# Retention of two sequences side by side in a fused retention and feed-forward kernel

## Chip, cores, metric

One NeuronCore of a Trainium2 chip. The metric is the device time of one execution in microseconds (us). An interval is a 95% interval of the ratio of two kernels.

## The reference

Eight sequences of 576 tokens, 8 heads of 64, go through retention; the result, 4608 tokens of 512 numbers, goes through a feed-forward layer with a squared ReLU.

```python
scores = q @ k.T / sqrt(64)              # per sequence and head
ret    = scores * gamma ** (i - j)       # for i >= j, else 0
x      = ret @ v                         # heads side by side: (4608, 512)
h      = maximum(x @ w_in, 0)            # (4608, 2048)
out    = (h * h) @ w_out                 # (4608, 512)
```

## The kernel before

A chunk is 128 tokens of one sequence (the fifth is 64). TensorE transposes k and q (`turn`), multiplies them (`scores`), and adds up the result from within the chunk and from a running state (`retain_a`, `retain_b`, `retain_c`). All of this runs in 64*64 or 64*128 tiles of TensorE. The results fill blocks of 512 tokens, and each block after the first goes through the first feed-forward product in 28 steps (`ffn_in`: four times seven block products, whose sums VectorE forms). A step is four matmul calls, which the profile shows as 8 records of 128x256: each call leaves two records. The steps of older blocks stand between the parts of retention:

```python
# main loop, from the sixth chunk on
retain_a(i - 1)
turn(i)              # k and q of chunk i
ffn(i - 1, 0)        # some 3 or 4 feed-forward steps
retain_b(i - 1)
scores(i)
retain_c(i - 1)
ffn(i - 1, 1)        # some 3 or 4 more
load(i + 3)
```

In `turn`, ScalarE copies kT out of PSUM, and VectorE takes out qT and multiplies it by the decay in the same instruction:

```python
nc.vector.tensor_tensor(to, p[:, :n_h, j, :, :], dq[...], op=ALU.mult)
```

The second product (`o_a`, `o_b`, `o_c`) follows when all retention is done.

## Time and profile before

| | before |
|---|---|
| time, median | 995.3 us |
| span of the profiled run | 991.7 us |
| TensorE busy / idle | 973.5 / 18.2 us |
| first block's products end | 104.3 us |
| second product starts at about | 560 us |
| time at half TensorE clock | 3.9 us |

The prediction shows the page, the stretches and a timeline. The view of TensorE's waits adds the following (what waited, for what: us in total, times, the longest). A wait for "issue" is one that no semaphore explains.

```profile
PE x_ps L436 <- ACT u_sb L474: 3.4, 4, 1.8
...
PE x_ps L471 <- issue: 1.3, 1, 1.3
...
PE t_ps L387 <- DVE q_ld L377: 0.6, 1, 0.6
```

### The profile page before, as it was taken

The numbers are of one execution on the slowest core, as the hardware profiler recorded it, in microseconds if no ns is written. First come the engines' busy times: TensorE is split into PE (matmuls) and PEld (weight loads), VectorE is DVE, ScalarE is ACT, GpSimd is POOL, SyncE is SP. The second block draws the span as 40 slices with busy tenths as digits, with TensorE's granted clock in tenths as the row PEclk, the third lists the DMA queues.
The fourth block names the chain that finished last, engine by engine and source line by source line (L and its number), as shares of the span: only waits on it lengthen the run. The fifth ranks groups of instructions, "written<-read, shape, count | busy, mean of one in ns | idle before, by whom it ended". The sixth has DMA issues, their size and how long they took to land.

```text
span 991.7 us, 24441 instructions
## 1 busy us (share of the span) xinstructions
PE 973.5 (98%) x10532; PEld 869.5 (88%) x10532; DVE 748.6 (75%) x1427; ACT 190.4 (19%) x462; POOL 81.6 (8%) x85
## 2 busy tenths in 40 slices
PE   7899999999999999999999999999999999999998
PEld 7655688888888888888888889999999999999998
DVE  4688696567878888897886777777777777777765
ACT  3444222222222222223221010000000000000000
POOL 3100011111111111111111000000000000000000
PEclk9999999999999999999999999999999999999999
DMA  9984657665696878769458999675673757556351
GB/s 205 250 239 143 174 172 208 162 175 176 187 311 199 223 234 260 224 209 283 142 212 297 404 389 348 235 283 163 230 268 148 265 197 270 192 213 216 126 212 44
DMA packets 187676, 220.40 MB, mean 222 GB/s; under 512 B 119216, under 2 KB 137648, under 8 KB 178608
## 3 DMA queue, kind: packets, MB, share of 16 engines
q1 hardware_dynamic: 185456, 218.31, 67.8%
q8 instruction: 83, 1.36, 0.6%
q10 hardware_dynamic: 2112, 0.52, 0.2%
q14 instruction: 25, 0.20, 0.1%
HBM read 129.41 MB, written 89.39 MB: 221 GB/s over the span
## 4 chain that ended last, share of the span: by engine, by line
PE 91%; DVE 5%; DMA 1%; SPq 1%; issue 1%; ACT 1%; DVEq 0%; ACTq 0%
PE o_b L866 17%; PE h_b L595 16%; PE o_c L866 11%; PE o_a L866 11%; PE h_a L595 10%; PE h_c L595 10%; PE h_ps L559 5%; PE x_ps L436 3%; PE t_ps L387 2%; PE sc_ps L415 2%; PE x_ps L471 2%; DVE room L602 1%; PE u_ps L439 1%; DMA w<-in_moe_w_in_dram 1%; DMA w<-in_moe_w_out_dram 0%
## 5 line engine op out<-in xcount | busy, mean ns | idle before, releaser
L595 PE MATMUL h_b<-room,w 128*128 128x256 f32 x736 | 177.2, 383 | 1.2 <-DVE room L520 0.9
L595 PEld LDWEIGHTS h_b<-room,w 128*128 128x128 f32 x736 | 137.2, 190 | 21.4 <-PE t_ps L387 1.1
L866 PE MATMUL o_b<-w,room 128*128 128x128 f32 x1168 | 144.5, 275 | 0.2 <-DVE room L817 0.2
L866 PEld LDWEIGHTS o_b<-w,room 128*128 128x128 f32 x1168 | 137.2, 192 | 0.5 <-DVE room L817 0.4
L866 PE MATMUL o_c<-w,room 128*128 128x128 f32 x1008 | 123.0, 275 | 0.0
L866 PEld LDWEIGHTS o_c<-w,room 128*128 128x128 f32 x1008 | 117.7, 192 | 0.0
L595 PE MATMUL h_c<-room,w 128*128 128x256 f32 x480 | 114.4, 381 | 0.0
L595 PE MATMUL h_a<-room,w 128*128 128x256 f32 x448 | 107.6, 383 | 0.0
L595 PEld LDWEIGHTS h_c<-room,w 128*128 128x128 f32 x480 | 90.4, 190 | 12.6
L595 PEld LDWEIGHTS h_a<-room,w 128*128 128x128 f32 x448 | 83.7, 190 | 11.8
L866 PE MATMUL o_a<-w,a 128*128 128x128 f32 x688 | 85.6, 275 | 0.0
L866 PEld LDWEIGHTS o_a<-w,a 128*128 128x128 f32 x688 | 81.2, 192 | 0.1
L612 POOL TENSOR_TENSOR room<-room 128x512 f32<-128x512 f32 x32 | 35.2, 1100 | 438.2 <-ACT room L611 370.6
L602 DVE SCALAR_TENSOR_TENSOR room<-room 128x512 f32<-128x512 f32 x96 | 68.1, 710 | 3.3
L880 ACT COPY r<-o_a 128x128 f32<-128x128 f32 x53 | 14.1, 266 | 271.7 <-PE o_a L866 241.2
L559 PE MATMUL h_ps<-room,w 128*128 128x512 f32 (+1 forms) x160 | 60.1, 526 | 2.5 <-DVE w L228 1.7
L614 DVE TENSOR_TENSOR room<-h_b,room 128x512 f32<-128x512 f32 x32 | 22.1, 690 | 46.9 <-PE h_b L595 46.9
L436 PEld LDWEIGHTS x_ps<-ret,v_ld 64*64 64x64 f32 x1152 | 40.4, 136 | 15.9 <-issue 11.7
L436 PE MATMUL x_ps<-ret,v_ld 64*64 64x64 f32 x1152 | 50.0, 226 | 3.5 <-ACT u_sb L474 3.4
L559 PEld LDWEIGHTS h_ps<-room,w 128*128 128x128 f32 x160 | 30.3, 196 | 24.6 <-issue 19.1
L424 POOL TENSOR_TENSOR v_ld<-v_ld,dv 128x512 f32<-128x512 f32 (+1 forms) x40 | 42.8, 1075 | 63.5 <-DMA v_ld<-in_v_dram 58.6
L876 DVE TENSOR_TENSOR small<-o_b,small 128x128 f32<-128x128 f32 x62 | 18.1, 292 | 38.4 <-PE o_b L866 38.4
(109 smaller groups left out, 1377.4 us busy)
## 6 DMA issues: line engine op xcount, KB each, us to landing
g_dram<-room SPq DMA_DIRECT2D x32, 1792.0 KB, 7.7
a<-g_dram SPq DMA_DIRECT2D x43, 1024.0 KB, 7.1
room<-g_dram SPq DMA_DIRECT2D x20, 1024.0 KB, 6.4
w<-w_dram SPq DMA_DIRECT2D x7, 1792.0 KB, 13.0
out_dram<-room SPq DMA_DIRECT2D x17, 512.0 KB, 3.4
w<-in_moe_w_in_dram SPq DMA_DIRECT2D x16, 512.0 KB, 6.1
w<-in_moe_w_out_dram SPq DMA_DIRECT2D x16, 512.0 KB, 4.1
v_ld<-in_v_dram SPq DMA_DIRECT2D x31, 256.0 KB, 4.4
```

The lines of the kernel that those rows point to most:

```text
L387: nc.tensor.transpose(p[:, h, j, hp, :], loaded[i][j][rows(h), 2 * hp:2 * hp + 2, :], ident[rows(h), rows(h)])
L415: nc.tensor.matmul(sc[e][rows(h), hp, :], lhsT=kT[rows(e), hp, t], rhs=qT[rows(e), hp, t], start=True, stop=True, skip_group_check=True)
L424: nc.gpsimd.tensor_tensor(vs[:cs], vs[:cs], dv[:cs, :, ci:ci + 1].to_broadcast([cs, H, D]), op=ALU.mult)
L436: own.append(lambda hp=hp, e=e, b=b: nc.tensor.matmul(x_at(hp, b, h), lhsT=s["vs"][rows(h), 2 * hp + b, :], rhs=s["ret"][rows(h), e, hp, : ...
L471: nc.tensor.matmul(x_at(hp, b, h), lhsT=u[rows(e), hp, :], rhs=s["qT"][rows(e), hp, CH * h:CH * h + CH], start=clears(b, hp // 2), stop=Fa ...
L559: nc.tensor.matmul(p.rearrange("p h t -> p (h t)"), lhsT=w[:, c, :], rhs=xT[0][:, c, lo * HT:hi * HT], start=(c == 0), stop=(c == N_DM - 1))
L595: nc.tensor.matmul(p[:, mm, :], lhsT=w[:, c, :], rhs=xs[n][right][:, c, :], start=(j in OPENS and mm == 0 and c == 0), stop=(j in CLOSES a ...
L602: nc.vector.scalar_tensor_tensor(t, t, 0.0, t, op0=ALU.max, op1=ALU.mult)
L612: nc.gpsimd.tensor_tensor(g["A11"], g["A11"], g["A11"], op=ALU.mult)
L614: nc.vector.tensor_tensor(g["A22"], p, p15, op=ALU.add)
L866: nc.tensor.matmul(p, lhsT=s["lefts"][left][:, m, :], rhs=w_out[j][:, m, WO_SLOT[right], :], start=(i in OPENS and m == 0), stop=(i in CLO ...
L876: nc.vector.tensor_tensor(s["u2"], p, s["p1"], op=ALU.add)
```

## The change

The intent is to switch between retention and feed-forward half as often. A "visit" is the same chunk of two sequences; their results share PSUM banks, so evictions are half as many and twice as wide. q is multiplied by its decay per token before the transposes, so that no table of decays by column is needed and qT is a plain copy. The order of the tokens in a block changes, so the output is stored in pieces of 128 or 64 rows. The core of the diff:

```diff
-    chunks = [(b, ci, ci * C, min(C, S - ci * C)) for b in range(B) for ci in range(NCH)]
+    visits = [(b, ci, ci * C, min(C, S - ci * C)) for b in range(0, B, 2) for ci in range(NCH)]
...
-                nc.vector.tensor_tensor(to, p[:, :n_h, j, :, :], dq[...], op=ALU.mult)
+            (nc.vector.tensor_copy if j == 0 and i < N_EARLY else nc.scalar.copy)(to, p[:, :n_h, j, :, :])
...
+    for i in range(N_EARLY, N_V + 1):
+        if i > N_EARLY:
+            if i < N_V:
+                turn(i, 0)               # first sequence of visit i
+            retain_a(i - 1)              # both sequences
+            if i < N_V:
+                turn(i, 1)               # second sequence
+            ffn(i - 1, 0)
+        if i + 1 < N_V:
+            load(i + 1, "q")
+        if i > N_EARLY:
+            retain_b(i - 1)              # both
+        if i < N_V:
+            scores(i)                    # both
+        if i > N_EARLY:
+            retain_c(i - 1)              # both
+        if i + 1 < N_V:
+            load(i + 1, "k")
+            load(i + 1, "v")
+        ffn(i - 1, 1)
+        if i + 1 < N_V:
+            scale_q(i + 1, nc.vector)
```

Cut: the early visits, which get the same order by hand; first-block products at half width, which go; and the stores.

## The prediction

> **What bounds the kernel now.** I read the page's sums and slices first, then the chain that ended last, then the stretches, the waits of TensorE, and last a timeline of one round of the middle part.
>
> ```profile
> span 991.7 us, 24441 instructions
> PE 973.5 (98%) x10532; PEld 869.5 (88%) x10532; DVE 748.6 (75%) x1427; ACT 190.4 (19%) x462; POOL 81.6 (8%) x85
> PE 91%; DVE 5%; DMA 1%; SPq 1%; issue 1%; ACT 1%; DVEq 0%; ACTq 0%
> ```
>
> TensorE is busy for 98% of the span and carries 91% of the chain that ended last. It waits for almost nothing; the table of stretches (us, TensorE busy) says where the 18 us of idle time lie:
>
> ```profile
> 0.00:46.00 46.00, 35.98 (x739) 30.86 (x740) 23.28 (x44) 18.09 (x38) 12.14 (x20) 0.96 0.91 219
> 104.00:537.00 433.00, 428.86 (x5369) 364.22 (x5368) 344.67 (x572) 106.88 (x235) 60.91 (x57) 1.00 0.70 212
> 560.00:992.00 432.00, 428.00 (x3684) 423.55 (x3683) 315.83 (x704) 36.23 (x130) 3.12 (x3) 1.00 0.63 228
> ```
>
> 10 us are in the start. The middle, where retention of later chunks is woven into the first feed-forward products, idles 4 us of 433; VectorE (third figure) is at 80% there. From 560 us on only the second product runs, which the change leaves alone but for its stores. So nothing can be won by removing waits; only TensorE's own work, or its order, can move the time. Here is one round of the middle (start us, us, engine, line):
>
> ```profile
> 305.16 0.23 PE L436 MATMUL x_ps<-ret,v_ld 64*64 64x64 f32 x2
> 305.17 0.23 PE L439 MATMUL u_ps<-v_ld,k_ld 64*64 64x64 f32 x2
> 305.32 1.99 PE L595 MATMUL h_b<-room,w 128*128 128x256 f32 x8
> 307.16 1.89 PE L595 MATMUL h_c<-room,w 128*128 128x256 f32 x8
> 308.88 1.89 PE L595 MATMUL h_b<-room,w 128*128 128x256 f32 x8
> 310.70 0.27 PE L436 MATMUL x_ps<-ret,v_ld 64*64 64x64 f32 x2
> ...
> 311.33 0.46 PE L387 MATMUL t_ps<-ident,k_ld 64*128 64x64 f32 x4
> 311.62 0.41 PE L387 MATMUL t_ps<-ident,q_ld 64*128 64x64 f32 x4
> 311.97 1.99 PE L595 MATMUL h_a<-room,w 128*128 128x256 f32 x8
> ```
>
> The reader is to see two things. A feed-forward group between its like takes 1.72 us start to start (307.16 to 308.88), but 1.84 just after retention and 1.82 just before it. And the transposes of q start 0.29 us after those of k, waiting for nobody: they read q as it was loaded. Now VectorE over the same moment; the three feed-forward groups ended at about 310.77:
>
> ```profile
> 307.36 0.69 DVE L614 TENSOR_TENSOR room<-h_b,room 128x512 f32<-128x512 f32 x1 [1.71 <-PE h_b L595]
> 308.08 0.69 DVE L602 SCALAR_TENSOR_TENSOR room<-room 128x512 f32<-128x512 f32 x1
> 308.69 0.42 DVE L214 TENSOR_SCALAR w<-w 128x512 uint32<-128x512 uint32 x1
> ...
> 311.02 0.68 DVE L621 TENSOR_TENSOR room<-h_b,room 128x512 f32<-128x512 f32 x1
> 311.74 0.69 DVE L602 SCALAR_TENSOR_TENSOR room<-room 128x512 f32<-128x512 f32 x1
> 312.35 0.68 DVE L533 TENSOR_TENSOR room<-room 128x512 f32<-128x512 f32 x1
> 312.95 0.68 DVE L225 TENSOR_TENSOR w<-w,w 128x512 f32<-128x512 f32 x1
> 313.55 0.42 DVE L397 TENSOR_TENSOR qT<-t_ps,dq 128x256 f32<-128x256 f32 x1
> ```
>
> VectorE is never the bound, but it runs **behind** TensorE: it finishes the work of the last group 2.9 us after that group ended, and only then gets to q (L397). Nobody minds today, because L397 comes after the transposes and its result is wanted only after the next 3 or 4 groups.
>
> [...] retention runs in 64*64 and 64*128 tiles, the feed-forward in 128*128, and each border costs about 0.1 us on either side. [...] The trace has one such wait already, at the very start (0.6 us, transposes for the scaling of q at L377). [...] the copy of kT at 26.11 us starts when the transposes of q end, 0.3 us after those of k.
>
> **The change part by part.** (1) **Fewer borders.** Before, 35 chunks after the early ones have two calls of feed-forward steps each: 70 rounds of "out of 128*128 and back". After, 18 visits (2 to 19) have two each, 36 at most. 34 rounds go. One round costs 0.10 (group before) + 0.12 (group after) + about 0.09 (the last retention matmul starts 0.15 us before the feed-forward, where its cadence is 0.06) + 0.04 (the first pair) = 0.35 us. Gain: 34 x 0.35 = **12 us**. The switch between transposes and 64*64 products is as frequent as before per sequence pair (turn, retain, turn), so it gives nothing.
>
> (2) **Same TensorE work.** The count of transposes, scores, products and state updates per token is unchanged, and TensorE is the bound: 0 us.
>
> (3) **Half as many, twice as wide evictions.** ScalarE and VectorE save fixed costs (a 128x256 copy takes 375 ns, a 128x512 one 585), but ScalarE is busy 19% and VectorE isn't the bound: 0 us. ScalarE takes over the eviction of qT, 585 ns each.
>
> (4) **q scaled by tokens, on VectorE, ahead of the transposes.** This is the part that I weigh most. The multiply by decay moves from behind the transposes (L397, 686 ns) to in front of them (a 128x512 TENSOR_TENSOR out of SBUF, about 690 ns as L377 at the start took 0.69), and it is issued after the last step of the second feed-forward call, just ahead of the next visit's transposes. Over 30 turns between 110 and 520 us I took the moment when VectorE was done with everything ahead of L397, from the end of the last feed-forward group: 0.1 to 4.7 us, median 2.4. By the order of the changed code I worked out on which product each second call ends: mostly on the fifth of seven (7 of 17), where VectorE is least behind: an addition, a square and one piece of the conversion of w_out, as at 307.36, done at 309.1, which is 1.8 us after the group's end at 307.3. Scaling then ends at 1.8 + 0.65 = 2.4 to 2.5; the transposes of q could have begun at 0.3. Stall: 2.1 to 2.2 us. For the other ten, 2.4 + 0.65 - 0.3, about 2.8 us. Mean 2.5 us x 17 visits (3 to 19) = **43 us**, all on TensorE's path[...].
>
> (5) **One buffer for q, two for k and v.** k of the next visit but one can load only when the current visit's last state update is done, six transfers in a row of 0.6 to 1.3 us issue each, 4.8 us median to landing. The first half lands about 7 us later; a half of 7 steps gives 12 us, but the halves beside the 64-token visits have 3 or 4 steps, 5 to 7 us. Estimate: 3 visits x 1.5 us more = 4 us, on top of (4).
>
> (6) **One transpose buffer, used twice a visit.** The second half's transposes wait for two ScalarE copies of the first half, 1.25 us; the products between take 2 x 0.63 us. About even: estimate 0.1 us x 17 = 2 us.
>
> (7) **Start.** x of the first block is ready at about 41 us now; I estimate 34 after, from the chain transposes, evictions, scores, mask of four sequence-chunks. But four half-width products and more were done before that (8 half groups by the trace, six of them ahead of 46 us), and these halves go: at full rate that is 11 us of TensorE. It comes out even, with 5 us of doubt. (8) **Tail.** More, smaller stores in the second product; SyncE has room, the last stores are of 128 rows as before: 0.
>
> Sum: 995 - 12 + 43 + 4 + 2 = 1032. Where VectorE has less to do (the last blocks, with w_out converted) the stall shrinks by 0.6; I take **1028 us**.
>
> **The rivals.** First: the stall is small, because the pieces fall so that VectorE is idle at the ends of the halves. For it: 5 of the 30 turns had VectorE done within 1.12 us, and the pace has been tuned to end on the product with the least behind it. Against it: even there the addition and the square of the last group must come first, which leaves no less than 0.07 + 0.7 + 0.65 + 0.65 - 0.3, about 1.7 us. Then 995 - 12 + 29 + 4 = 1016. Second: the borders are all that counts, and q is ready in time: 983 to 988. It needs the scaling to be off TensorE's path, and the order of the program speaks against that. Third: VectorE or the loads become the bound, with k, v and q late at every visit since there is only one buffer of q: each visit loses 4 us, 1045 to 1050. Transfers' share of 0.70 in the middle makes room, and the load of q has 10 to 15 us; unlikely.
>
> **Range and chances.** The stall per visit is the large term; 1.4 to 3.3 us makes 24 to 56, and the start gives 5 either way. Range 1006 to 1046. Within 2% ends at 1015; it takes a stall under about 1.6 us, or a start that gains some 10 us. Faster by 2% takes a mechanism that I don't see.
>
> **What would show it.** In the changed trace TensorE's waits should name the scaling of q on VectorE as the releaser ahead of the transposes of q, some 17 times, 2 to 3 us each, 35 to 45 us in total; TensorE's share should fall to about 95%. The groups of 128x256 products should show half as many of the 1.99 us kind. Part 560 us to the end should keep its length of 432 us. I am wrong if that wait is absent or under 20 us in all, if waits on loads of q or k are larger, or if the first block's products end over 8 us earlier or later than the 104 us of now.

## More of the kernel before

The runs were made on several chips, each beside the kernel before, whose median lay between 994.2 and 997.3 us; ratios allow for that.

## The result

The changed kernel takes 1139.7 us (median of 4 runs, 1137.7 to 1142.0), against 995.5 beside it. The ratio is 1.145 (1.142 to 1.147). Ratios are the mean time of one kernel's runs over that of the other's of the same rounds, so not quite the ratio of the medians. It is slower, as predicted, but by 144 us, not 33, and far outside the range.

The page and the stretches of the changed kernel (the columns of a stretch: us, then busy time of TensorE, its weight loads, VectorE, ScalarE and GpSimd, the granted clock of TensorE, the transfers' share, GB/s):

```profile
span 1140.3 us, 24565 instructions
...
PE 1026.3 (90%) x10636; PEld 910.5 (80%) x10636; DVE 764.2 (67%) x1408; ACT 197.6 (17%) x422; POOL 89.2 (8%) x82
```

```profile
46.00:104.00 58.00, 45.76 (x448) 23.66 (x449) 33.38 (x56) 20.72 (x36) 2.91 (x2) 0.87 0.50 141
...
300.00:400.00 100.00, 86.37 (x1041) 73.87 (x1040) 65.23 (x102) 23.24 (x41) 13.18 (x11) 0.88 0.56 171
...
708.00:1140.00 432.00, 427.89 (x3684) 423.46 (x3682) 316.27 (x704) 36.26 (x130) 3.12 (x3) 1.00 0.63 229
```

The part from 708 us to the end is as long as the 432 us of before, so the smaller stores cost nothing. All is lost ahead of it, in two forms. TensorE idles for 114.0 us in place of 18.2, which is 95.8 more. And it is **busy** for 52.8 us more, with the same useful matmuls (104 more records: 136 more of idle matmuls at the start, and 32 fewer since the half-width products became whole ones): the granted clock is 0.87 to 0.97 in every stretch up to 700 us, where in the kernel before it was 0.96 in the first 46 us and 1.00 after them. The two add up to the 148.6 us between the spans of the two profiled runs.

The waits of TensorE:

```profile
PE t_ps L391 <- DVE q_ld L381: 52.4, 19, 5.7
PE u_ps L446 <- issue: 16.9, 4, 5.4
PE x_ps L443 <- issue: 16.3, 4, 5.4
PE h_c L602 <- issue: 6.3, 2, 3.2
```

So there are three things to explain.

**The wait for the scaling of q** is the one predicted. Here is one of the 19 (weight loads left out):

```profile
588.07 0.47 PE L391 MATMUL t_ps<-ident,k_ld 64*128 64x64 f32 x8
588.17 0.69 DVE L621 TENSOR_TENSOR room<-h_b,room 128x512 f32<-128x512 f32 x1 [0.81 <-PE h_b L602]
588.90 0.69 DVE L609 SCALAR_TENSOR_TENSOR room<-room 128x512 f32<-128x512 f32 x1
589.51 0.68 DVE L227 SCALAR_TENSOR_TENSOR w<-w,w 128x512 uint32<-128x512 uint32 x1
590.11 1.29 DVE L381 TENSOR_TENSOR q_ld<-q_ld,dv 128x512 f32<-128x512 f32 x2
590.85 0.69 PE L391 MATMUL t_ps<-ident,q_ld 64*128 64x64 f32 x8 [2.32 <-DVE q_ld L381]
```

The reader is to see the queue of VectorE: the addition, the square and the conversion that belong to the last feed-forward step come first, then the scaling, and only then, after 2.32 us, does TensorE go on.

**The waits for "issue"** were in nobody's forecast. One of them:

```profile
566.60 1.11 PE L421 MATMUL sc_ps<-qT,kT 64*64 64x64 f32 x64
...
568.12 0.28 PE L443 MATMUL x_ps<-ret,v_ld 64*64 64x64 f32 x3
...
573.82 0.26 PE L443 MATMUL x_ps<-ret,v_ld 64*64 64x64 f32 x1 [5.42 <-issue]
```

TensorE stops in the middle of one loop of equal matmuls whose inputs are all there, and goes on 5.4 us later. The count of records from one such gap to the next tells what it is:

```profile
369.80:411.40 41.60, 34.39 (x382) 29.19 (x381) 28.15 (x45) 9.37 (x16) 5.08 (x4) 0.87 0.51 155
411.40:454.30 42.90, 37.38 (x381) 31.82 (x382) 27.66 (x44) 8.72 (x16) 6.10 (x4) 0.86 0.44 150
```

Each stretch has 763 matmuls and weight loads. With the semaphore instructions of TensorE that the trace lists (151 among 21,426, so about 5), that is 768, or 3 x 256. Counted in the trace, all ten long "issue" gaps lie at the same remainder, 193, when the place in TensorE's instruction stream is divided by 256; so does the one "issue" wait of the kernel before, and every one in the runs below. The page's queues show 83 transfers of instructions of 1.36 MB in all, 16 KB each, and TensorE's 21,426 instructions are 83.7 times 256 (in `rep4`, below, 106 transfers stand against 106.5). So the counts fit one transfer for each block of 256 instructions. In the kernel before no block after 30 us took less than 6.4 us, and no "issue" gap is there. In the changed kernel `retain_b`, `scores` and `retain_c` of two sequences are up to 384 instructions in a row (weight loads counted), and a block that falls inside runs in 1.9 us. Ten blocks ran in under 3.6 us, and each was followed by a gap: the next one began 3.7 to 7.6 us after the start of the short one.

The transfers of these blocks show the cause directly. In the example the transfer begins inside the gap (at 571.3 us), takes 0.95 us, and TensorE goes on 1.6 us after its end. With the transfers taken in order, one for each block from the third on, TensorE began no block of any run (1091 of them) earlier than 1.2 us after the end of its transfer, and all 69 "issue" waits of all runs ended 1.2 to 1.7 us after one. So TensorE waited for the block.

Eight of the ten transfers began 4.2 to 5.2 us after the short block did, and all eight met full transfer engines (a busy share of 1.0 in the next 1.5 us); the other two began after 0.8 and 2.2 us and met a share of 0.6. Over all 48 borders between 50 and 700 us, 15 transfers began after more than 3.4 us, and 13 of them met full engines; but at 9 borders with full engines the transfer began earlier than that, twice even ahead of the border. At the 26 borders where the engines had room, 22 transfers began 0.1 to 2.4 us after it. That full engines delay the transfer is likely, not shown. The 1.8 MB store of the feed-forward result was issued 1.6 to 2.8 us ahead of eight of the nine short blocks after 110 us.

**The half clock.** The records of the granted clock have 145 us at 0.5, against 3.9 before, in spells of 3.41 us or two or three times that. They follow idle stretches: 23 of the 24 gaps of 2.0 us or more have one beginning within 3 us of their end, or running into it. So have some of 1.7 to 2.0 us, but not every one: the wait of 1.72 us that ended at 227.0 us has one, that of 1.71 us at 263.9 us has none. After the gap that ended at 429.5 us the clock is 0.5 from 430.2 to 437.0, and a feed-forward group that takes 1.89 us takes twice that:

```profile
432.58 3.78 PE L602 MATMUL h_c<-room,w 128*128 128x256 f32 x8
```

### The profile page after: what moved, and what is told of

Same layout as the page of the kernel before. It is cut to its first block, busy times and chain, and to the rows that moved or that the text cites. A ratio compares the mean times of both kernels' runs of the same rounds, so it can differ in the third digit from the quotient of the medians.

```text
span 1140.3 us, 24565 instructions
## 1 busy us (share of the span) xinstructions
PE 1026.3 (90%) x10636; PEld 910.5 (80%) x10636; DVE 764.2 (67%) x1408; ACT 197.6 (17%) x422; POOL 89.2 (8%) x82
## 3 DMA queue, kind: packets, MB, share of 16 engines
q8 instruction: 83, 1.36, 0.5%
## 4 chain that ended last, share of the span: by engine, by line
PE 64%; DVE 4%; issue 4%; DMA 2%; ACT 0%; DVEq 0%; SPq 0%
PE o_b L881 15%; PE o_c L881 10%; PE o_a L881 10%; PE h_b L602 10%; PE h_c L602 8%; PE h_a L602 6%; PE x_ps L443 2%; DMA w<-w_dram 1%; PE t_ps L391 1%; PE x_ps L482 1%; PE sc_ps L421 1%; DMA g_dram<-room 1%; DVE room L609 1%; PE u_ps L446 1%; DVE q_ld L381 1%
## 5 line engine op out<-in xcount | busy, mean ns | idle before, releaser
L602 PE MATMUL h_b<-room,w 128*128 128x256 f32 x736 | 182.4, 392 | 6.2 <-DVE room L530 6.2
L602 PEld LDWEIGHTS h_b<-room,w 128*128 128x128 f32 x736 | 145.9, 199 | 33.1 <-issue 11.0
L602 PE MATMUL h_c<-room,w 128*128 128x256 f32 x480 | 131.6, 422 | 3.2 <-issue 3.2
L602 PEld LDWEIGHTS h_c<-room,w 128*128 128x128 f32 x480 | 100.5, 213 | 20.5 <-issue 3.4
L625 DVE TENSOR_TENSOR room<-h_c,room 128x512 f32<-128x512 f32 x32 | 22.0, 689 | 96.3 <-PE h_c L602 96.3
L391 PE MATMUL t_ps<-ident,q_ld 64*128 64x64 f32 x288 | 22.6, 279 | 52.4 <-DVE q_ld L381 52.4
L567 PE MATMUL h_ps<-room,w 128*128 128x512 f32 x128 | 64.5, 659 | 2.5 <-ACT room L504 1.1
L446 PE MATMUL u_ps<-v_ld,k_ld 64*64 64x64 f32 x1024 | 50.3, 259 | 16.9 <-issue 16.9
L446 PEld LDWEIGHTS u_ps<-v_ld,k_ld 64*64 64x64 f32 x1024 | 44.2, 169 | 24.7 <-issue 24.7
L391 PEld LDWEIGHTS t_ps<-ident,q_ld 64*128 64x128 f32 x288 | 17.9, 185 | 55.1 <-DVE q_ld L381 55.1
```

The lines of the kernel that those rows point to most:

```text
L391: nc.tensor.transpose(p[:, h, j, hp, :], loaded[i][name][rows(h), s_, 2 * hp:2 * hp + 2, :], ident[rows(h), rows(h)])
L446: grow.append(lambda hp=hp, e=e, b=b: nc.tensor.matmul(u_ps[0][rows(e), s_, hp, :], lhsT=ks[rows(1 - h), s_, 2 * hp + e, :], rhs=vs[rows(1 ...
L567: nc.tensor.matmul(p.rearrange("p h t -> p (h t)"), lhsT=w[:, c, :], rhs=xT[0][:, c, :], start=(c == 0), stop=(c == N_DM - 1))
L602: nc.tensor.matmul(p[:, mm, :], lhsT=w[:, c, :], rhs=xs[n][right][:, c, :], start=(j in OPENS and mm == 0 and c == 0), stop=(j in CLOSES a ...
L625: nc.vector.tensor_tensor(g["S3"], p, u2, op=ALU.add)
```

## The experiments

Theory A: three costs, in this order. Waits for the scaling of q, gaps where a block of instructions comes too late, and the half clock that both bring about. Rivals: the waits only move to another engine; the gaps are stores or buffers that the trace doesn't name; the half clock comes from long stretches of small tiles. Eleven kernels ran, all correct. The table has the changed kernel's sums beside theirs; "issue" is the sum of all TensorE waits for it. `rep4` ran twice, the others four or six times.

| run | us (median) | ratio to before | scaling wait | issue | TensorE idle | half clock |
|---|---|---|---|---|---|---|
| before | 995.5 | 1 | 0.6 | 1.3 | 18.2 | 3.9 |
| changed | 1139.7 | 1.145 | 52.4 | 39.7 | 114.0 | 145 |
| qpool | 1070.4 | 1.075 (1.071-1.078) | 9.2 | 37.3 | 75.1 | 78 |
| short | 1094.3 | 1.095 (1.089-1.100) | 40.8 | 5.8 | 79.3 | 118 |
| both | 1048.0 | 1.052 (1.049-1.054) | 9.1 | 5.4 | 54.7 | 60 |
| rep4 | 1071.9 | 1.075 (1.072-1.079) | 0.6 | 25.8 | 41.9 | 19 |
| tok1 | 1121.3 | 1.126 (1.124-1.129) | 80.7 | 2.4 | 95.7 | 103 |
| phase | 1021.1 | 1.026 (1.023-1.028) | 9.6 | 4.2 | 40.7 | 49 |
| align | 1020.5 | 1.026 (1.021-1.031) | 8.4 | 4.0 | 43.3 | 32 |
| misalign | 1036.0 | 1.039 (1.034-1.044) | 8.4 | 20.4 | 54.4 | 41 |
| best | 1017.3 | 1.021 (1.017-1.025) | 0.6 | 2.7 | 33.2 | 27 |
| best2 | 1008.0 | 1.013 (1.010-1.015) | 0.5 | 4.7 | 33.2 | 21 |
| best3 | 994.2 | 0.999 (0.997-1.001) | 0.7 | 3.9 | 23.1 | 19 |

### q scaled on GpSimd (qpool)

```diff
-        ffn(i - 1, 1)
-        if i + 1 < N_V:
-            scale_q(i + 1, nc.vector)
+        # called four steps before the end of the second call
+        ffn(i - 1, 1, (lambda: scale_q(i + 1, nc.gpsimd)) if i + 1 < N_V else None)
```

> The changed kernel, but q of the next visit is scaled on GpSimd, four steps before the end of the second feed-forward call, in place of VectorE after its end (main loop only; the two early visits as they were). Theory: three things cost the 145 us: the waits of the q transposes for VectorE (52.4 us, some 43 of them in the main loop), gaps at every 256th instruction of TensorE inside dense bursts (39.5 us), and the half clock that follows such idle stretches (145 us at half clock, about 53 us of TensorE's busy time). This run takes the first away: the waits for the scaling fall to about 9 us (the early ones), the gaps stay at 35 to 45 us, the half clock falls by a third; 1060 to 1085 us. Rival, that the waits only move (to GpSimd, or the evictions behind the transposes): 1110 us or more. Rival, that the half clock comes from long stretches of small tiles and not from idling: the time falls by no more than the 43 us, to about 1097.

It took 1070 us, as expected. The waits fell by 43 us, the time by 69: the half clock went with them (145 to 78 us), which speaks against small tiles as its cause. The issue gaps stayed. The run changes the engine and the moment of the scaling together; what the earlier moment alone would do on VectorE was not run.

### Short bursts (short), and both edits (both)

```diff
             retain_b(i - 1)
+            between(2)        # two feed-forward steps, if there are any
         if i < N_V:
             scores(i)
         if i > N_EARLY:
+            between(2)
             retain_c(i - 1)
```

> The changed kernel, but two feed-forward steps stand between the products with the state and the scores, and two more between the scores and the last products, so that at most 128 short instructions of TensorE (weight loads counted) follow each other in that half; q is scaled as in the changed kernel. Theory of instruction supply (a block of 256 instructions that runs in under 3.5 us is followed by a gap, since the next block comes 4.7 to 7.6 us after the start of the one before): the gaps of 39.5 us fall under 8 us; 2 more borders a visit cost 17 x 2 x 0.35 = 12 us; the half clock falls by a third; 1080 to 1105 us. Rival, the gaps are waits that the trace doesn't show (a store or a load that holds the tiles): gaps stay over 25 us, time 1140 to 1155.

> Both edits. Theory: waits for the scaling about 9 us, gaps under 8 us, half clock under 50 us, most of it in the first 140 us; 1010 to 1045 us. If the half clock had its cause in the small tiles and not in the idling, it would stay over 80 us and the time over 1050.

In `short` the gaps fell from 39.7 to 5.8 us and the time to 1094. Two things had not been expected: the waits for the scaling fell too (from 52.4 to 40.8 us), so not all of the gain is the gaps', and the half clock fell by a fifth, not by a third. And a wait came in their place: the steps that moved ahead are missing behind `retain_c`, where k of the next visit but one has to land.

```profile
PE t_ps L391 <- DVE q_ld L381: 40.8, 15, 5.7
PE t_ps L391 <- DMA k_ld<-in_k_dram: 16.3, 8, 5.2
PE x_ps L443 <- issue: 4.9, 3, 2.0
```

With both edits it took 1048 us, 3 more than the range: the same wait for k (18.1 us) had not been expected, and the half clock was 60 us, not under 50.

### Dense bursts in the kernel before (rep4)

```diff
-        for hp in range(HP):
+        for hp in [hp for _ in range(4 if i > N_EARLY else 1) for hp in range(HP)]:   # scores
```

> The kernel before, but each chunk's scores after the early ones are computed four times in place of once (same result), so that its bursts grow from 192 to 384 short instructions. Theory of instruction supply: the work alone costs 3 x 0.47 us x 35 = 50 us; half of the bursts hold a full block of 256, so some 15 gaps of 3 to 5 us appear at every-256th places, with half clock after them: 1100 to 1160 us. Rival, bursts don't matter and the gaps belong to the visits' buffers: 1040 to 1050 us and no gaps.

In the kernel before, with no visits and no scaling of q, eleven new gaps appeared, every one at a border of 256 instructions, 24.5 us together. The time is 1072 us, between the two expectations: the theory's gaps are there, but shorter (1.0 to 4.6 us), 7 of the 17 blocks under 3.6 us had their successor at once, and there was little half clock. The transfers tell why: six of these seven blocks began 1.9 to 4.1 us after the transfer of their successor had begun, and the seventh, of 3.6 us, was just long enough. Nor does a gap need a block under 3.6 us: two of the eleven (1.3 us each) follow blocks of 5.3 and 5.5 us whose successor's transfer began only after 4.7 us.

### One part of the change alone (tok1)

```diff
 # kernel before, from the sixth chunk on; qT is then a ScalarE copy
+            if i < N_CH:
+                scale_q(i, nc.vector)
             retain_a(i - 1)
             turn(i)
```

> The kernel before with one part of the change alone: from chunk 5 on q is scaled by tokens on VectorE after the second feed-forward call, ahead of the next transposes, and qT is evicted by ScalarE; one sequence at a time as before. Theory: the scaling lies on TensorE's path whatever the visits do. By the backlog of VectorE in the kernel before (median 2.5 us after retention begins) less the 0.9 us of products and k transposes that now stand ahead, plus 0.6 of scaling: about 2.2 us x 35 chunks = 77 us of waits for it, some half clock besides; 1060 to 1110 us, and no gaps at every 256th instruction. Rival, the waits come only with visits: under 1015 us.

```profile
PE t_ps L387 <- DVE q_ld L377: 80.7, 34, 4.4
```

34 waits of 2.4 us on average, where 35 of 2.2 were expected: the backlog of VectorE, read from the profile of before, gives the wait. The time, 1121 us, is above the range, because the half clock (103 us) had been given too little: TensorE was busy for 49 us more than before, about half of that time. Its bursts are those of the kernel before, so this half clock doesn't come from denser small tiles.

### The pace three steps earlier (phase), and the borders moved (align, misalign)

`phase` is `qpool` with one constant changed, so that the store of g is issued some five steps ahead of a burst. `align` is `qpool`, and `misalign` is `phase`, each with idle matmuls at the start, which move the 256-borders and nothing else.

```diff
-    LAST = -2
+    LAST = -5                 # phase, misalign
     warm(6, True)
+    warm(21, False)           # align: 168 instructions; misalign: 15, 120 instructions
```

> As the run with GpSimd scaling (1070 us), but the pace is three steps earlier, so that the halves end on the second product of seven and the 1.8 MB store of g is issued some five steps ahead of a dense burst, not one. Theory: in the changed kernel the next block of instructions started its transfer 4 to 5 us after the boundary when the DMA engines were full, and about 1 us after when they were not; so the gaps at every 256th instruction get shorter: from 38 us to under 25 in about as many gaps, and the time falls to 1045 to 1062 us. Rival, the gap's length has nothing to do with the store: 38 us of gaps and 1065 to 1078 us.

> As the run with GpSimd scaling (1070 us, store of g right ahead of the bursts), but 21 more rounds of idle matmuls, 168 instructions, stand at the very start, where TensorE waits for its first loads anyway. They only move the borders of the blocks of 256 instructions against the dense bursts. By the instruction order of that run's trace, 2 blocks after 110 us then run in under 3.6 us, in place of 7. Theory of instruction supply: gaps at block borders fall from 38 us to under 15, with some half clock; 1030 to 1050 us. Rival, the gaps come from stores, buffers or waits that the trace doesn't show: no change, 1065 to 1078 us.

> As the run with the earlier pace (1021 us, store of g some five steps ahead of the bursts, 2 short blocks by its instruction order), but 15 more rounds of idle matmuls, 120 instructions, at the start. By the instruction order 13 short blocks result. Theory: 10 to 13 gaps come back. If full DMA engines are what makes a gap 4 to 5 us long, these are 1 to 3 us each, 15 to 30 us together, and the time is 1035 to 1060 us; if the gap's length doesn't depend on the store, they are 4 to 5 us each, over 45 us together, and the time is over 1070 us. If blocks don't matter: 1021 us.

`phase` took 1021 us, better than its theory, but for a reason mixed with luck: the borders had moved too, so that 3 blocks ran in under 3.6 us where `qpool` had 9. The other two runs take this apart. `align` leaves the store at the bursts and **adds** 168 instructions of no use, and it is 50 us faster than `qpool`: 4.0 us of gaps are left. The two largest "issue" waits of `qpool`, then the largest of `align`:

```profile
PE x_ps L443 <- issue: 16.0, 4, 5.1
PE u_ps L446 <- issue: 9.5, 2, 4.8
```

```profile
PE h_b L602 <- issue: 2.7, 1, 2.7
```

No store, buffer or semaphore of the program was touched, and the first block's products end at 126.0 us in both runs, so the blocks of instructions are the cause. `misalign` brings gaps back (4.2 to 20.4 us) at the pace that has the store out of the way; the time rises by 15 us, which is also what its theory gave (1035 to 1060 us). The two largest of these waits:

```profile
PE u_ps L446 <- issue: 9.1, 4, 4.4
...
PE x_ps L443 <- issue: 8.1, 3, 4.3
```

Nine gaps of 0.5 us or more, 2.2 us each on average, against 3.7 in `qpool` (37.3 us in 10): shorter, as the theory of full engines expected, but fewer than the 10 to 13 foreseen, and three of the nine lie in the start. Of the 13 short blocks after 110 us five had no gap at all; in each of the five the successor's transfer had begun 1.4 to 4.1 us before the block did. That the store sets the length of a gap is supported, not shown; two of these nine still took 4.3 and 4.4 us.

### What the order is worth (best, best2, best3)

`best` is `both` with the four steps in between taken from the first call, so that k has its time, and q of the early third visit on GpSimd. `best2` is `phase` with the latter. `best3` adds one feed-forward step between the first sequence's transposes and `retain_a`:

```diff
-        count = max(1, int(want) - done[0])
+        count = max(1, int(want) - done[0] - (4 if half == 0 else 0))   # best only
...
     scores(1, (1,))
+    scale_q(2, nc.gpsimd)                                               # all three
...
                 turn(i, 0)
+            if steps and steps[0][0] > 0:                               # best3 only
+                step()
             retain_a(i - 1)
```

> As the run with both edits (1048 us), but the four steps that stand between the parts are taken from the first feed-forward call, so that the second keeps its length and k has time to land, and the early second visit's q is scaled on GpSimd too. Theory: the 18 us of waits for k fall under 5, the 9 us of early waits for the scaling vanish with some of the half clock after them: 1010 to 1030 us. It has as many borders of tiling mode as the kernel before, so nothing of the 12 us is won, and it isn't expected to beat 995. Rival, that one buffer pair for k is the limit whatever the order: waits for k over 12 us, 1035 us or more.

> As the run with the earlier pace (1021 us), bursts whole, and the early second visit's q scaled on GpSimd too. Theory: the 9 us of early waits for the scaling go and some of the half clock of the start with them; the first block's products end at 113 to 120 us in place of 129, the middle keeps its length; 1001 to 1013 us. If the start's loss lay elsewhere (x of the first block late, products at half width gone), 1016 or more.

> The same, and one feed-forward step between the first half's transposes and the products after them, so that the second half's transposes don't wait for the evictions of the first (12 us of waits for qT). Theory: those waits fall under 4 us, 17 more borders cost 6 us: 996 to 1010 us, a few us under the run beside it; no version is expected to beat the kernel before by over 1%.

The times of `best` and `best2` came out as expected; `best3` ended 2 us below its range. In `best` the wait for k fell from 18.1 to 5.8 us, not quite under the 5 expected. In `best2` the first block's products end at 114.6 us, not 129.3. In `best3` the wait for the evictions of qT fell from 12.3 to 3.5 us, and the time is 14 us lower, where a few us had been expected:

```profile
PE t_ps L391 <- ACT qT L397: 3.5, 4, 1.5
PE t_ps L391 <- DMA k_ld<-in_k_dram: 3.1, 6, 1.2
PE x_ps L443 <- issue: 2.7, 2, 1.8
```

`best3` equals the kernel before (0.999, 0.997 to 1.001). No version beat it: `best` is slower by about 2% (whether by more than that is unclear), `best2` by 1.3%. Part of `best3`'s result is luck of the borders: by the instruction order of its trace, a shift by 120 instructions would turn 2 short blocks after 110 us into 12 (counted, not run).

## Why the prediction was wrong, point by point

- **Fewer borders, 12 us won.** The count was about right: the trace has 39 rounds out of 128*128 tiles where there were 76, and 17 groups of the 1.99 us kind where there were 64. What they are worth was not isolated. `best3`, with a third round per visit, is busy for 968.1 us against 973.5 before, in spite of 15 us more at half clock, so TensorE's own work did shrink; by how much each part of the change shrank it is not measured.
- **"Same TensorE work ... 0 us": the step that failed.** The count of retention's instructions was unchanged, but the step took for granted that they arrive in time and run at full clock. Instead TensorE waited 38 us for late blocks (39.7 less 1.3) and was busy for 52.8 us longer: 91 of the 112 us between the forecast and the result. Putting retention together in longer bursts is the very thing that the change was made for. It was counted as a gain, and it made the late blocks.
- **q scaled ahead of the transposes, 43 us.** Right, in mechanism and size: the main loop's 16 waits sum to 43.4 us (1.7 to 5.7 us each, where 2 to 3 were forecast). That such a wait holds up all of TensorE was assumed, with one wait of 0.6 us in the profile of before to show it; here all of the 52.4 us is idle time of TensorE. The rest of the 52.4 lies in the early visits, which the sum had left out, and the consequence was missed: nearly every wait of 2 us or more is followed by half clock (23 of the 24 gaps of that length). In `qpool`, 43 us of waits taken away were worth 69 us of time.
- **Start "comes out even".** Wrong by 36 us: the first block's products end at 140.8 us, not 104.3. Four waits for the scaling make 19 us of it (4.2, 4.2, 5.7, 4.8), and spells of half clock up to 126 us sum to 38 us, whose half is another 19 (an estimate; both are contained in the sums above).
- **Loads (4 us), one transpose buffer (2 us), tail (0).** Close: 1.4 us of waits for k, 3.5 us for evictions, 432 us of second product before and after. The sums at the heads of blocks wait 6.2 us, which nothing had foreseen.
- **The rivals** held three ways in which the known waits could differ in size. None held a new kind of cost. Yet both parts of the failed step had left a trace in the profile of before: one "issue" wait of 1.3 us, in the start, where short matmuls stand densest (279 records from 10 to 20 us), and one dip of the clock to 0.83 between 40 and 50 us, after the waits of the start.

What stays open: how the busy time splits between half clock and borders, why `best3` still reaches the end of its first block 7 us later than before, why some transfers of instructions begin ahead of the border and others up to 5 us after it, and why one gap of 3.1 us had no half clock after it.

## What to carry to other kernels

An operation that was moved from behind a TensorE instruction to in front of it cost the backlog of its engine here (in `tok1` 2.4 us on average, 34 times), though that engine was busy for only 75% of the span; issued four steps early on GpSimd, which was busy for 8%, it left none of the main loop's 43.4 us of waits. Many short matmuls in a row outran the supply of instructions here (256 in 1.9 us, then a wait of up to 5.4 us for the next block), so count the instructions of a burst: with 192 in a row (weight loads included) the kernel before had no gap after its start, with 384 in a row both the changed kernel and `rep4` had ten or more. Putting longer matmuls in between took most of the gaps away (39.7 us of them fell to 5.8 in `short`). Look for "issue" gaps at the same remainder of 256 (193 here). Where TensorE is the bound, a gap can cost more than its length (43 us of waits taken away were worth 69 here); and where a time jumps on an edit that should do nothing, check where the block borders have moved (168 idle instructions made 50 us of difference in `align`).
